# Attention units feeding a two-layer network: eight units scale their coarse probabilities on ScalarE, and a planner orders all work with a transfer rate of 400 GB/s

## The chip, the cores and the metric

One core of one Trainium2 chip. The metric is the device time of one execution in microseconds (us); the median of three runs is compared. Five engines work side by side, each through its own queue in a fixed order: TensorE (PE, with its weight loads PEld), VectorE (DVE), ScalarE (ACT), GpSimd (POOL) and SyncE (SP), which here issues every transfer.

## The reference

Attention over 4 batches of 8 heads (576 positions, 64 wide) is the sum of two parts: a coarse one on sums of four neighbours, and a local one with a band mask. Its output goes through a network of 512 to 2048 to 512 with the function h * tanh(softplus(h)).

```python
q_d = q.reshape(B, H, Sd, factor, D).mean(axis=3)      # factor = 4, k_d and v_d alike
out_up = np.repeat(sm_attn(q_d, k_d, v_d), factor, axis=2)
mask = np.abs(pos[:, None] - pos[None, :]) < factor
scores = np.where(mask, scale * np.matmul(q, k.transpose(0, 1, 3, 2)), -1e9)
x = out_up + softmax(scores) @ v                       # then to (2304, 512)
h = x @ w_in
g = h * np.tanh(np.log1p(np.exp(h)))                   # h itself above 20
return g @ w_out
```

## The kernel before

**Units.** Two heads make a unit; there are 16, named by batch b and pair p (0_0 to 3_3). A unit loads `qk` and `vv`, sums its q and k over fours on DVE (L347), and makes coarse scores `sc` (L362) and local scores `sl` (L397, for batches 0 and 1 with the mask added by a matmul, L392). The coarse exponentials are three ACT instructions (L369); the division by their sum is either three ACT instructions (L377, for units listed in `AMUL`) or one DVE instruction (L380). The local exponentials are either nine small ACT instructions with their sums (L407, units in `AEXP`, after two DVE steps L403 and L405) or one long ACT instruction (L417) between DVE steps L414, L415 and L418. Then PE transposes (`at` L443, `pt` L467, L473), multiplies with the coarse values (`pvo` L456, which needs POOL's sums `vd`, L430 and L432) and with the local values (`pve`, `pvo`, L482), and DVE and ACT put the sum into `x` as two fp32r parts (L495, L507, L509).

**Slots.** The network runs in 96 slots: a chunk c of 384 rows times one block f of 128 of the 2048 columns. A slot is 12 matmuls into `h` (L569), a chain between ACT and DVE (L583, L584, L586, L587, L589, L590, L593, L595) that ends with `g`, and 9 matmuls into three accumulators `acc` (L608, three for each). The first 32 slots run over chunks 0 and 1 together, chunk 1 behind chunk 0 by `LEAD` blocks; there the weights `wi` and `wo` of each block are loaded into `stg` and turned into two parts, with two ACT and four DVE instructions each (L541, L542, L544, L547, L550, L551). Chunks 2 to 5 use the weights that lie there, and units of batches 2 and 3 run among their slots, with one buffer each for `qk` and `vv`. The first six units have three buffer sets and a fourth, shared with all later units; the slots' PSUM is opened when those six are done.

**Order.** Nothing of it is written by hand. A planner in the kernel walks through a model of the engines, takes the ready operation with the lowest priority number, and writes each engine's order down. Priorities come from `ATT`, `UNIT`, `WPRI`, `VOFF`, `WDMA` (units, weights, transfers) and `LAG` (how many slots behind h the matmuls into acc come: slots below 20, below 60, the rest). `RATE` is the bandwidth by which it expects transfers to land:

```python
op("sp", P * 18 * 512 / RATE, lambda: nc.sync.dma_start(vv(), self.vv[b, p]), w=[vv], prio=pv_)
...
op("pe", 700, mm2, r=[*gi, wo], w=[a_], cols=1536, prio=s + LAG[(s >= 20) + (s >= 60)] - 0.5 + 0.1 * i)
```

Where PE has nothing ready, the planner may put in matmuls on constants (L695, into `warm` or into the unused end of an h buffer). On the chip the order is fixed, and each instruction waits for its own data.

Of the kernel before, what the change touches and what calls it, by code (L numbers as in the profile page):

```python
# [19 lines left out]
P = 128  # L20
BIG = 1e30
CH = 384
LAG = (3.5, 5.5, 5.5)
FA = 5
SETS = 3
ATT = {0: (-900, 20), 1: (-46, 10.0), 2: (5, 13.0), 3: (34, 5.5)}
WPRI = (9.1, 2.2, 7.7)
UNIT = {(0, 0): -3, (0, 1): -5, (0, 2): -2, (0, 3): -3, (1, 0): 5, (1, 1): -1, (1, 3): 1, (2, 0): -2, (2, 1): -1, (2, 2): 5, (2, 3): 2, (3, 0): 4, (3, 1): 2, (3, 2): 3, (3, 3): -2, (1, 2): -2}
WARM = True
NPRO = 6  # L30
STICK = 15
VOFF = 40
WDMA = 0
PIPE0 = (1, 0, 1)
PIPE1 = (1, 0, 1)
LEAD = 1
PMASK = (0, 1)
AMUL = ((0, 2), (1, 2))
AEXP = ((0, 1), (0, 2), (0, 3), (1, 1))
NMISH = (3, 2)  # L40
TAIL = 0
TICK, BUSY, PACE = 3413.3, 3060, 1.6
KW = 38
RATE = 280.0
DQ = 2500
ENGINES = ("pe", "act", "dve", "pool", "sp")
LATENCY = {"pe": (0, 197, 196, 272, 634), "act": (215, 143, 142, 170, 645), "dve": (240, 128, 127, 180, 620),
# [31 lines left out]
class Plan:  # L79
# [6 lines left out]
    def buf(self, group, tag, shape, dtype=F32, bufs=1, name=None):  # L86
        return Buf(self, group, tag, shape, dtype, bufs, name or f"{tag}_{len(self.ops)}")
# [183 lines left out]
def dve(n, fast=False):  # L271
    return 69 + (0.52 if fast else 1.042) * n


def act(n, psum=False, extra=0):
    return (52 if psum else 94) + 0.833 * n + 93 * extra
# [6 lines left out]
class Kernel:  # L283
# [45 lines left out]
    def attention(self, b, p, sb, ps, L, loose):  # L329
# [15 lines left out]
        qk, qkd = buf("qk", [P, 2, S + 6]), buf("qkd", [P, 2 * C])  # L345
        op("sp", P * 8 * (S + 6) / RATE, lambda: nc.sync.dma_start(qk(), self.qk[b, p]), w=[qk])
        op("dve", dve(2 * S), lambda: nc.vector.tensor_reduce(  # L347
# [26 lines left out]
        op("dve", 88, lambda: nc.vector.reciprocal(cst()[:, 3], cst()[:, 2]), w=[cst])  # L374
        if (b, p) in AMUL:
            for m in range(3):
# [24 lines left out]
        wide = lambda i: lst()[:, i, :, None].broadcast_to([P, T, KW])  # L401
        if (b, p) in AEXP:
            op("dve", dve(T * KW), lambda: nc.vector.tensor_reduce(out=lst()[:, 0], in_=sl3(), op=ALU.max, axis=AX.X),  # L403
# [20 lines left out]

        pv_ = pl.prio + VOFF
        vv, vd = buf("vv", [P, 18, P]), buf("vd", [72, 2, P])
        op("sp", P * 18 * 512 / RATE, lambda: nc.sync.dma_start(vv(), self.vv[b, p]), w=[vv], prio=pv_)
        vw = lambda: vv()[:, :10].rearrange("p (t f) c -> p t f c", f=2)
# [95 lines left out]
    def load_w(self, f):  # L524
# [6 lines left out]
        for nm, src in (("wi", wi), ("wo", wo)):  # L531
            pl.prio = prio + (WPRI[2] if nm == "wo" else 0)
            st_ = pl.buf("stg", "stg", [P, 512, 2], I32, self.nstg, f"stg_{nm}{f}")
# [4 lines left out]
            tmp = pl.buf("stg", "tmp", [P, 512], I32, 1, f"tmp_{nm}{f}")  # L538
            op("sp", P * 4096 / RATE, lambda st_=st_, src=src: nc.sync.dma_start(
                st_().rearrange("p (c f) w -> p c (f w)", c=4), src), w=[st_], prio=pl.prio + WDMA)  # L540
            op("act", act(512), lambda hf=hf: nc.scalar.activation(hf(), hf(), AF.Copy, scale=2.0 ** -112), w=[h])  # L541
# [14 lines left out]
    def slot(self, s, c, f):  # L556
# [46 lines left out]
        for i in range(3):  # L603
# [7 lines left out]
            gi = [g] if len(parts) == 1 else [(g, 2 * i), (g, 2 * i + 1)]  # L611
            op("pe", 700, mm2, r=[*gi, wo], w=[a_], cols=1536, prio=s + LAG[(s >= 20) + (s >= 60)] - 0.5 + 0.1 * i)
            if not last:
# [8 lines left out]
            r0 = c * CH + i * P  # L622
            op("sp", P * 2048 / RATE, lambda r0=r0, o=o: nc.sync.dma_start(self.out[r0:r0 + P, :], o()[:, :512]), r=[o], prio=s + 1)

    def run(self, ctx):
# [28 lines left out]
        for b in (0, 1):  # L654
            for p in range(self.NPAIR):
                if len(units) == NPRO:
                    break
                units.append((ATT[b][0] + ATT[b][1] * p + UNIT.get((b, p), 0), self.attention(
                    b, p, sets[len(units) % len(sets)], ("props", "attps"),
# [100 lines left out]
```

## Time and profile before

| what | value |
|---|---|
| median of 3 runs | 531.98 us (529.66 to 532.99) |
| the profiled execution | 531.69 us |
| its span, first to last instruction | 529.9 us |
| PE busy, share of the span | 511.8 us, 97% |
| DVE busy | 325.3 us, 61% |
| ACT busy | 356.8 us, 67% |

Matmuls are pipelined, so a busy PE is not PE at its peak: the matmuls on constants count as busy, and so does work at the lower clock. Shares over the whole span mix three stages: units alone, units and weights beside slots, and slots alone.

### The profile page before, as it was taken

To read this page: it belongs to the slowest core of one execution; us is meant where nothing else is said; L and a number is where in the kernel's file an instruction comes from. 1 tells how busy PE (TensorE), PEld (TensorE's weight loads), DVE (VectorE), ACT (ScalarE), POOL (GpSimd) and SP (SyncE) were. 2 spreads that over 40 slices of the span, in tenths; PEclk is the share of its full clock that TensorE was granted. 3 is DMA by queue.
4 is the path that set the end of the run, shared out by engine and by line. 5 is a ranking of instruction groups with operands and counts; after the bars stand their busy time and mean duration, and the time that the engine had idled before them with its cause. 6 is when DMAs were issued, how large, how long until landed. Compare 5 with 4: busy or idle time off the path is not lost.

```text
span 529.9 us, 11811 instructions
## 1 busy us (share of the span) xinstructions
PE 511.8 (97%) x4919; PEld 440.0 (83%) x4919; DVE 325.3 (61%) x686; ACT 356.8 (67%) x865; POOL 39.9 (8%) x54
## 2 busy tenths in 40 slices
PE   7889989999999999999999999999999999999997
PEld 3667777989899898878888788798989899898985
DVE  6677999999999633677745978543333333334242
ACT  3666778898889867667566566656566665666653
POOL 5430121000000000011200211100000000000000
PEclk9798999999999999999999999999999999999999
DMA  8763465434554000433303333100001000010001
GB/s 343 288 266 122 141 212 208 160 119 160 162 157 160 0 1 17 149 137 136 137 1 131 138 139 112 42 1 1 0 0 61 1 0 1 0 62 0 1 0 59
DMA packets 11861, 50.66 MB, mean 96 GB/s; under 512 B 1312, under 2 KB 1312, under 8 KB 9760
## 3 DMA queue, kind: packets, MB, share of 16 engines
q1 hardware_dynamic: 11808, 49.91, 26.4%
q8 instruction: 38, 0.62, 0.5%
q14 instruction: 15, 0.12, 0.1%
HBM read 45.19 MB, written 4.72 MB: 94 GB/s over the span
## 4 chain that ended last, share of the span: by engine, by line
PE 63%; DVE 4%; issue 1%; ACT 1%; POOL 0%
PE h L569 29%; PE acc L608 28%; PE pve L482 1%; PE sl L397 1%; PE sc L362 1%; PE pvo L456 1%; PE pt L467 1%; PE at L443 1%; PE pvo L482 1%; DVE g L595 1%; DVE mH L590 0%; DVE A L380 0%; DVE lst L418 0%; POOL vv L430 0%; DVE stg_wo L547 0%
## 5 line engine op out<-in xcount | busy, mean ns | idle before, releaser
L569 PE MATMUL h<-x,wi 128*128 128x384 f32 x1152 | 222.9, 340 | 1.9 <-DVE mH L590 1.6
L608 PE MATMUL acc<-wo,g 128*128 128x512 f32 x864 | 216.7, 395 | 0.5 <-DVE g L595 0.5
L569 PEld LDWEIGHTS h<-x,wi 128*128 128x128 f32 x1152 | 200.8, 188 | 14.7 <-DVE mH L590 6.8
L608 PEld LDWEIGHTS acc<-wo,g 128*128 128x128 f32 x864 | 160.5, 188 | 30.5 <-DVE g L595 0.9
L584 DVE TENSOR_SCALAR mA<-mA 128x384 f32<-128x384 f32 (+1 forms) x98 | 35.6, 364 | 95.3 <-ACT mA L583 95.3
L595 DVE SCALAR_TENSOR_TENSOR g<-mH,g 128x384 fp32r<-128x384 f32 (+1 forms) x98 | 56.2, 575 | 57.9 <-ACT g L593 57.9
L583 ACT ACTIVATE mA<-h 128x384 f32<-128x384 f32 (+1 forms) x98 | 46.8, 480 | 56.5 <-PE h L569 55.2
L586 ACT ACTIVATE mA<-mA 128x384 f32<-128x384 f32 (+1 forms) x98 | 50.6, 517 | 33.3 <-DVE mA L584 32.9
L593 ACT ACTIVATE g<-mH 128x384 fp32r<-128x384 f32 (+1 forms) x98 | 50.2, 514 | 16.2 <-PE acc L608 14.9
L587 ACT ACTIVATE mA<-mA,one 128x384 f32<-128x384 f32 (+1 forms) x98 | 59.0, 603 | 1.5
L590 DVE SCALAR_TENSOR_TENSOR mH<-mA,h 128x384 f32<-128x384 f32 (+1 forms) x98 | 53.1, 543 | 3.1 <-ACT mA L589 0.9
L589 ACT ACTIVATE mA<-mA 128x384 f32<-128x384 f32 (+1 forms) x98 | 50.4, 516 | 2.3
L430 POOL TENSOR_TENSOR vv<-vv 72x512 f32<-72x512 f32 x16 | 21.2, 1325 | 291.9 <-PE acc L608 176.4
L369 ACT ACTIVATE A<-sc,cst 128x144 f32<-128x144 f32 x48 | 17.9, 377 | 15.2 <-DVE cst L367 15.1
L482 PEld LDWEIGHTS pve<-PT,vv 38*64 38x64 f32 x640 | 21.1, 136 | 6.3 <-issue 3.4
L482 PE MATMUL pve<-PT,vv 38*64 38x32 f32 x640 | 23.0, 221 | 2.4 <-issue 2.4
L347 DVE TENSOR_REDUCE qkd<-qk 128x288 f32<-128x1152 f32 x16 | 21.5, 1343 | 4.6 <-DMA qk<-in_qk_dram 4.5
L397 PEld LDWEIGHTS sl<-qk 64*32 64x32 f32 x1152 | 13.2, 114 | 6.8 <-issue 5.3
L495 DVE TENSOR_TENSOR x<-pve,xd 128x320 f32<-128x320 f32 x16 | 7.8, 489 | 17.5 <-PE pve L482 17.3
L695 PE MATMUL warm<-ident 128*128 128x512 bf16 x56 | 17.0, 433 | 1.6 <-POOL ident masks.py:199 1.6
L482 PE MATMUL pvo<-PT,vv 38*64 38x32 f32 x512 | 18.4, 222 | 0.0
L507 ACT ACTIVATE x<-x 128x384 fp32r<-128x384 f32 (+1 forms) x32 | 12.4, 437 | 8.7 <-DVE x L495 8.7
(74 smaller groups left out, 460.6 us busy)
## 6 DMA issues: line engine op xcount, KB each, us to landing
vv<-in_vv_dram SPq DMA_DIRECT2D x16, 1152.0 KB, 5.8
qk<-in_qk_dram SPq DMA_DIRECT2D x16, 582.0 KB, 5.7
stg_wi<-in_w_in_dram SPq DMA_DIRECT2D x16, 512.0 KB, 3.4
stg_wo<-in_w_out_dram SPq DMA_DIRECT2D x16, 512.0 KB, 3.7
out_dram<-o SPq DMA_DIRECT2D x18, 256.0 KB, 2.1
```

Of the source, the lines that this page charges most:

```text
L347: op("dve", dve(2 * S), lambda: nc.vector.tensor_reduce(out=qkd().rearrange("p (a t) -> p a t", a=2), in_=qk()[:, :, 3:3 + S].rearrange("p ...
L482: nc.tensor.matmul(o_()[64 * h:64 * h + 64, c0:c0 + 32], vw()[64 * e:64 * e + KW, t // 2, f, 64 * h:64 * h + 64], PT()[64 * e:64 * e + KW, ...
L569: nc.tensor.matmul(h()[:, :CH], w()[:, a, kt * P:(kt + 1) * P], x()[:, b_, :], start=kt == 0 and j == 0, stop=kt == 3 and j == 2)
L583: op("act", act(n, True), lambda o_=o_: nc.scalar.activation(A()[:, o_], h()[:, o_], AF.Exp), r=[h_], w=[a_])
L584: op("dve", dve(n, True), lambda o_=o_: nc.vector.tensor_scalar(A()[:, o_], A()[:, o_], float(math.exp(20.0)), 1.0, op0=ALU.min, op1=ALU.a ...
L586: op("act", act(n), lambda o_=o_: nc.scalar.activation(A()[:, o_], A()[:, o_], AF.Square), w=[a_])
L587: op("act", act(n, False, 1), lambda o_=o_: nc.scalar.activation(A()[:, o_], A()[:, o_], AF.Ln, bias=self.one), w=[a_])
L589: op("act", act(n), lambda o_=o_: nc.scalar.activation(A()[:, o_], A()[:, o_], AF.Exp, scale=-1.0), w=[a_])
L590: op("dve", dve(n), lambda o_=o_: nc.vector.scalar_tensor_tensor(out=H()[:, o_], in0=A()[:, o_], scalar=0.5, in1=h()[:, o_], op0=ALU.subtr ...
L593: op("act", act(n), lambda o_=o_: nc.scalar.activation(g()[:, 0, o_], H()[:, o_], AF.Copy, scale=-2.0), r=[x_], w=[one])
L595: op("dve", dve(n), lambda o_=o_: nc.vector.scalar_tensor_tensor(out=g()[:, 1, o_], in0=H()[:, o_], scalar=-2.0, in1=g()[:, 0, o_].bitcast ...
L608: nc.tensor.matmul(a_(), g()[:, a, i * P:(i + 1) * P], wo()[:, b_], start=first and j == 0, stop=last and j == 2)
```

## The change

Only constants at the head of the file are changed. The first eight units (batches 0 and 1) all scale their coarse probabilities on ACT (`AMUL`), two units instead of four make their local exponentials in small ACT instructions (`AEXP`), and the numbers that set priorities and the transfer rate are others, so that the planner writes another order. The instructions of a slot, of a weight block and of the units of batches 2 and 3 stay the same.

```diff
-LAG = (3.5, 5.5, 5.5)
+LAG = (2.5, 5.0, 4.5)
...
-ATT = {0: (-900, 20), 1: (-46, 10.0), 2: (5, 13.0), 3: (34, 5.5)}
-WPRI = (9.1, 2.2, 7.7)
+ATT = {0: (-900, 20), 1: (-46, 10.0), 2: (5, 13.0), 3: (-34.40956924936998, 8.52050951677553)}
+WPRI = (10.326569533908831, 2.2, 1.3072351415990624)
...
-VOFF = 40
-WDMA = 0
+VOFF = 10
+WDMA = 3
...
-LEAD = 1
+LEAD = 2
...
-AMUL = ((0, 2), (1, 2))
-AEXP = ((0, 1), (0, 2), (0, 3), (1, 1))
+AMUL = ((0, 0), (0, 1), (0, 2), (0, 3), (1, 0), (1, 1), (1, 2), (1, 3))
+AEXP = ((0, 0), (1, 2))
...
-RATE = 280.0
+RATE = 400.0
```

`UNIT` changes for (0, 0), (0, 2), (0, 3) and (3, 2). The matmuls on constants go from 56 to 33 (`warm`) and from 39 to 14 (into h).

**The head of SP's queue.** A name holds batch, pair and a running number: `vv1_2` is the vv of unit 1_2. Before:

```order
L346 DMA qk0_0_116<-in_qk_dram 128x1164
L346 DMA qk0_1_119<-in_qk_dram 128x1164
L427 DMA vv0_0_130<-in_vv_dram 128x2304
L346 DMA qk0_2_187<-in_qk_dram 128x1164
...
L427 DMA vv1_1_815<-in_vv_dram 128x2304
L539 DMA stg_wi0_905<-in_w_in_dram 128x1024
L427 DMA vv1_2_969<-in_vv_dram 128x2304
L346 DMA qk1_3_1068<-in_qk_dram 128x1164
L539 DMA stg_wo0_1103<-in_w_out_dram 128x1024
L539 DMA stg_wi1_1164<-in_w_in_dram 128x1024
```

and of the change:

```order
L346 DMA qk0_0_116<-in_qk_dram 128x1164
L427 DMA vv0_0_118<-in_vv_dram 128x2304
L346 DMA qk0_1_132<-in_qk_dram 128x1164
L427 DMA vv0_1_177<-in_vv_dram 128x2304
L346 DMA qk0_2_192<-in_qk_dram 128x1164
...
L539 DMA stg_wi0_624<-in_w_in_dram 128x1024
L539 DMA stg_wo0_640<-in_w_out_dram 128x1024
L427 DMA vv1_1_662<-in_vv_dram 128x2304
L539 DMA stg_wi1_742<-in_w_in_dram 128x1024
L427 DMA vv1_2_900<-in_vv_dram 128x2304
L346 DMA qk1_3_978<-in_qk_dram 128x1164
```

Each vv of the first units now stands straight behind its own qk and ahead of the next one's; wo0 and wi1 moved ahead of vv1_2, which waits for a buffer of unit 0_3.

**PE between the h of slot 8 and the first acc of slot 8** (`h9` is the h of slot 9, `g8` the g of slot 8). Before:

```order
L569 MATMUL h8_1780<-x3_1_963,wi3_1646 128x384 x3
L608 MATMUL acc0_1_1521<-wo3_1678,g5_1745 128x512 x3
...
L608 MATMUL acc2_2_1652<-wo2_1592,g6_1778 128x512 x3
L569 MATMUL h9_1841<-x0_0_449,wi5_1792 128x384 x3
...
L608 MATMUL acc0_0_1510<-wo4_1739,g7_1839 128x512 x3
L569 MATMUL h10_1877<-x0_1_491,wi4_1717 128x384 x3
...
L608 MATMUL acc0_1_1521<-wo4_1739,g7_1839 128x512 x3
L608 MATMUL acc0_2_1529<-wo4_1739,g7_1839 128x512 x3
L608 MATMUL acc2_0_1635<-wo3_1678,g8_1864 128x512 x3
```

and of the change:

```order
L569 MATMUL h8_1751<-x3_0_951,wi5_1697 128x384 x3
L608 MATMUL acc0_1_1431<-wo4_1679,g6_1748 128x512 x3
L608 MATMUL acc0_2_1444<-wo4_1679,g6_1748 128x512 x3
L569 MATMUL h9_1797<-x0_1_501,wi3_1524 128x384 x3
L569 MATMUL h9_1797<-x1_1_674,wi3_1524 128x384 x3
L608 MATMUL acc3_0_1629<-wo2_1484,g7_1794 128x512 x3
L569 MATMUL h9_1797<-x2_1_809,wi3_1524 128x384 x3
L569 MATMUL h9_1797<-x3_1_956,wi3_1524 128x384 x3
L608 MATMUL acc3_1_1642<-wo2_1484,g7_1794 128x512 x3
L608 MATMUL acc3_2_1652<-wo2_1484,g7_1794 128x512 x3
L569 MATMUL h10_1843<-x0_0_488,wi6_1788 128x384 x3
L608 MATMUL acc0_0_1388<-wo5_1742,g8_1832 128x512 x3
```

Before, eight acc rows and eight h rows lie between the last h8 and the first use of g8; now five acc rows and five h rows do.

**PE between the end of unit 2_0 and `pvo` of unit 2_1.** Before:

```order
L482 MATMUL pve2_0_3048<-PT2_0_3053,vv2_0_1515 64x32 x4
L362 MATMUL sc2_1_3101<-qkd2_1_3032 64x144 x6
L397 MATMUL sl2_1_3114<-qk2_1_2981 32x38 x36
L608 MATMUL acc32_2_3158<-wo0_1335,g32_2897 128x512 x3
...
L608 MATMUL acc32_0_2995<-wo2_1592,g34_3174 128x512 x3
L569 MATMUL h38_3198<-x0_2_1105,wi6_1850 128x384 x3
...
L443 MATMUL at1_2_1_3215<-ident_59,A2_1_3165 72x128 x3
L569 MATMUL h38_3198<-x2_2_1327,wi6_1850 128x384 x3
...
L569 MATMUL h39_3232<-x0_2_1105,wi7_1933 128x384 x3
L456 MATMUL pvo2_1_3240<-AT02_1_3220,vd2_1_3227 64x144 x2
```

and of the change:

```order
L482 MATMUL pve2_0_3005<-PT2_0_3010,vv2_0_1536 64x32 x4
L362 MATMUL sc2_1_3052<-qkd2_1_2965 64x144 x6
L397 MATMUL sl2_1_3064<-qk2_1_2931 32x38 x36
L569 MATMUL h37_2981<-x3_2_1547,wi5_1697 128x384 x3
L608 MATMUL acc32_0_2945<-wo1_1235,g33_2874 128x512 x3
...
L569 MATMUL h38_3140<-x0_2_1073,wi6_1788 128x384 x3
L569 MATMUL h38_3140<-x1_2_1156,wi6_1788 128x384 x3
...
L443 MATMUL at1_2_1_3159<-ident_59,A2_1_3114 72x128 x3
L569 MATMUL h38_3140<-x2_2_1373,wi6_1788 128x384 x3
L569 MATMUL h38_3140<-x3_2_1547,wi6_1788 128x384 x3
L456 MATMUL pvo2_1_3181<-AT02_1_3164,vd2_1_3169 64x144 x2
```

Before, five acc rows and five h rows of slots lie between the two; now three acc rows and five h rows do.

## Rows read from the trace of the kernel before

**Rows 1.** The page: busy time by engine, and two transfers by size and landing.

```profile
PE 511.8 (97%) x4919; PEld 440.0 (83%) x4919; DVE 325.3 (61%) x686; ACT 356.8 (67%) x865; POOL 39.9 (8%) x54
...
vv<-in_vv_dram SPq DMA_DIRECT2D x16, 1152.0 KB, 5.8
qk<-in_qk_dram SPq DMA_DIRECT2D x16, 582.0 KB, 5.7
```

**Rows 2.** Windows by stage: length, busy PE, PEld, DVE, ACT, POOL, clock, DMA, GB/s.

```profile
4.50:62.00 57.50, 51.37 (x1206) 36.64 (x1205) 44.25 (x105) 36.24 (x169) 15.42 (x22) 0.91 0.62 243
62.00:93.00 31.00, 28.07 (x384) 23.77 (x383) 30.25 (x62) 24.36 (x56) 5.30 (x4) 1.00 0.56 197
93.00:219.00 126.00, 125.94 (x631) 113.17 (x630) 95.62 (x192) 103.13 (x207) 0.00 (x0) 1.00 0.32 103
219.00:340.00 121.00, 117.46 (x1774) 99.03 (x1774) 86.96 (x188) 75.03 (x200) 15.39 (x14) 1.00 0.33 118
340.00:516.00 176.00, 176.00 (x884) 158.45 (x884) 64.44 (x132) 111.36 (x218) 0.00 (x0) 1.00 0.03 10
```

**Rows 3.** The same view, two stretches of 10 us.

```profile
10.00:20.00 10.00, 7.14 (x171) 5.30 (x169) 8.12 (x24) 9.06 (x50) 4.08 (x5) 1.00 1.02 418
20.00:30.00 10.00, 8.91 (x199) 6.92 (x200) 5.50 (x15) 5.41 (x26) 2.73 (x4) 0.66 0.53 202
```

**Rows 4.** Chain that ended last: start, length, what; two slots apart.

```profile
371.04 2.11 PE h L569 x12
...
379.44 2.11 PE h L569 x12
```

**Rows 5.** Timeline of PE: start, length, instruction, idle time before and releaser.

```profile
21.09 0.32 PE L482 MATMUL pve<-PT,vv 38*64 38x32 f32 x2 [2.42 <-issue]
...
39.35 0.46 PE L456 MATMUL pvo<-AT,vd 72*64 72x144 f32 x2 [1.80 <-issue]
...
46.09 0.25 PE L482 MATMUL pve<-PT,vv 38*64 38x32 f32 x2
...
65.07 1.32 PE L569 MATMUL h<-x,wi 128*128 128x384 f32 x6
...
93.22 4.47 PE L569 MATMUL h<-x,wi 128*128 128x384 f32 x24
```

**Rows 6.** Timeline of POOL: vv of units 0_3 and 1_2 landed just before.

```profile
21.65 1.27 POOL L430 TENSOR_TENSOR vv<-vv 72x512 f32<-72x512 f32 x1 [0.84 <-DMA vv<-in_vv_dram]
...
52.95 1.26 POOL L430 TENSOR_TENSOR vv<-vv 72x512 f32<-72x512 f32 x1 [13.87 <-DMA vv<-in_vv_dram]
```

**Rows 7.** Groups by line of DVE in 0 to 93 us: busy us, mean ns.

```profile
L509 DVE TENSOR_TENSOR x<-x,x 128x384 fp32r<-128x384 f32 (+1 forms) x16 | 8.1, 545 | 0.1
...
L380 DVE TENSOR_TENSOR A<-A,cst 128x432 f32<-128x432 f32 x6 | 3.6, 596 | 0.1
...
L415 DVE TENSOR_TENSOR L_att<-sl,lst 128x342 f32<-128x342 f32 x4 | 2.0, 502 | 0.0
L418 DVE TENSOR_REDUCE lst<-L_att 128x9 f32<-128x342 f32 x4 | 2.0, 495 | 0.0
```

**Rows 8.** Groups by line and shape of ACT, whole span.

```profile
L407 ACT ACTIVATE L_att<-sl,lst 128x38 f32<-128x38 f32 x36 | 10.3, 296 | 0.0
...
L377 ACT ACTIVATE A<-A,cst 128x144 f32<-128x144 f32 x6 | 2.0, 407 | 0.5 <-DVE cst L374 0.5
```

**Rows 9.** Tile vv in 205 to 345 us: durations min/median/max, and landing.

```profile
L430 POOL TENSOR_TENSOR vv<-vv x7: 1282/1294/1382, 235.7 to 331.8; 72x512 f32<-72x512 f32 x7
L432 POOL TENSOR_TENSOR vd<-vv x7: 723/930/1043, 237.1 to 333.2; 72x256 f32<-72x256 f32 x7
...
DMA to landing us min/median/max: 5.0/5.2/7.0
```

**Rows 10.** Timeline of PE: the h of slot 12.

```profile
120.97 2.27 PE L569 MATMUL h<-x,wi 128*128 128x384 f32 x12
```

**Rows 11.** Timeline of DVE: the g of slot 12.

```profile
130.24 0.55 DVE L595 SCALAR_TENSOR_TENSOR g<-mH,g 128x384 fp32r<-128x384 f32 x1
```

More of the change, by code (lines that the diff above doesn't have):

```diff
@@ L22 @@
 CH = 384
-LAG = (3.5, 5.5, 5.5)
+LAG = (2.5, 5.0, 4.5)
 FA = 5
 SETS = 3
-ATT = {0: (-900, 20), 1: (-46, 10.0), 2: (5, 13.0), 3: (34, 5.5)}
-WPRI = (9.1, 2.2, 7.7)
-UNIT = {(0, 0): -3, (0, 1): -5, (0, 2): -2, (0, 3): -3, (1, 0): 5, (1, 1): -1, (1, 3): 1, (2, 0): -2, (2, 1): -1, (2, 2): 5, (2, 3): 2, (3, 0): 4, (3, 1): 2, (3, 2): 3, (3, 3): -2, (1, 2): -2}
+ATT = {0: (-900, 20), 1: (-46, 10.0), 2: (5, 13.0), 3: (-34.40956924936998, 8.52050951677553)}
+WPRI = (10.326569533908831, 2.2, 1.3072351415990624)
+UNIT = {(0, 0): 1, (0, 1): -5, (0, 2): 1, (0, 3): -1, (1, 0): 5, (1, 1): -1, (1, 3): 1, (2, 0): -2, (2, 1): -1, (2, 2): 5, (2, 3): 2, (3, 0): 4, (3, 1): 2, (3, 2): 4, (3, 3): -2, (1, 2): -2}
 WARM = True
```

## The prediction

> **What bounds the kernel now.** The page comes first: PE is busy 97% of the span and DVE 61% [rows 1], which looks like a PE limit throughout. The windows by stage correct that [rows 2, 3]. From 340 to 516 us PE is busy all the time and DVE a third of it: slots alone, nothing to win by an order. A pair of slots starts every 8.40 us there, a slot costs 4.2 us, its four h rows 2.11 us and its nine acc matmuls (three rows of 0.70) the rest [rows 4]. From 93 to 219 us PE is busy too (125.94 of 126.00). From 219 to 340 us it is idle for 3.5 us. What is lost lies ahead of 93 us. The first h starts only at 65.07 us and the first that runs on without a gap at 93.22 us [rows 5]. By then PE has done the eight first units, five h and ten acc rows. Many of the busy microseconds there are matmuls on constants.
>
> In that first stage DVE is what comes last. It is busy 44.25 of 57.5 us from 4.5 to 62 us and 30.25 of 31 us from 62 to 93 us [rows 2]: 74.5 us of work and 14.0 us of idling, nearly all of it early, and then a queue that never empties until weight block 3 is ready and the slots can run on. So the start is set by DVE's early idle time. It waits there for PE and ACT: PE stands 2.42 us in the middle of unit 0_0 and 1.80 us in unit 0_3, both with nothing but its own issue as releaser [rows 5], and behind the first of these the granted clock falls to 0.66 for 10 us [rows 3]. Unit 0_3 multiplies with its values at 46.09 us although its vv landed by 21.65 us [rows 5, 6]; unit 1_2 shares its buffer, so its vv lands only at 52.95 us, and wo0 and wi1 stand behind that transfer in SP's queue.
>
> **The change part by part.** *Scaling on ACT, fewer exponentials on ACT.* Up to weight block 3, six L380 go (6 x 0.596 = 3.6 us of DVE [rows 7]). Two units leave `AEXP` on balance: each gains L415 and L418 (1.0 us) and drops the short L405 (I take 0.2 us), +1.6 us together [rows 7]. ACT gets 18 more L377 (7.3 us) and loses 18 L407 (5.3 us and their sums) for two long L417 [rows 8]. It is busy 36.24 of 57.5 us there [rows 2], so it takes this, and its queue loses the long runs of nine L407 behind which other units waited. By DVE's order, weight block 3 is also reached with seven instructions fewer of x, weights and slots (two each of L509 and L584, one each of L542, L590 and L595); L509 is 0.545 us [rows 7], the others no longer, so I take 3.3 us. DVE's work to that point is 74.5 - 3.6 + 1.6 - 3.3 = 69.2 us.
>
> *The order of the first 93 us.* Transfers really land at the rate that the planner now assumes: 418 GB/s while the queue is full [rows 3], so 2.8 us for a vv of 1152 KB and 1.4 us for a qk of 582 KB [rows 1]. Since each vv goes ahead of the next qk, the second qk lands about 2.8 us later than before and the third at some 13 to 14.5 us, and DVE waits for it: I put 2.5 us. Unit 0_0 then multiplies with its values at about 20 us, since in the new order that stands behind the third unit's scores. From there a unit costs DVE some 5.5 us (up to 62 us it did seven units and one weight tile in 44.25 us [rows 2], about 6 each, and 0.6 us of that is L380), and transfers are ahead: unit 0_1 at 26, 0_2 at 31 and 0_3 at 36 us (before 46.09). Then vv of 1_2 goes out, lands 5.2 us later [rows 9] at some 42 us (before 52.95), and wo0 and wi1 no longer stand behind it. The first h starts near 50 us.
>
> So DVE's finish with block 3 is 4.5 us (its start) + 69.2 us + idle time. For the idle time I add 2.5 us for the third qk, 1 us at the first units, when only two are under way, and 2 us for unplanned PE stops of the kind that the trace shows: 5.5 us, against 14.0. That gives 79.2 us. PE has then done one h and three acc rows less than at 93.22 us before, 2.1 + 2.1 = 4.2 us. At equal work the start is at 83.4 us instead of 93.2: **9.8 us gained**. Ends: with 2 us idle 13.3, with 11 us (four fifths of before) 4.3; if all idle time stays it is 1.3.
>
> The Trainium skill's page "DMA: Bandwidth & Descriptors" (section "Where 436 GB/s comes from") has about 358 GB/s per core bind for reads from HBM; the trace's 418 GB/s disagrees. By that figure the first ten transfers, 8.3 MB, would end 3.3 us later (an estimate), and the gain would be nearer 7 us.
>
> *Behind the start.* With `LEAD` 2 block 4 is wanted a slot earlier; between blocks 3 and 4 DVE has 17 rows, some 8.5 us at half a microsecond each as L509's [rows 7], and PE eight h and five acc rows, 8 x 0.53 + 5 x 0.70 = 7.7 us: +1 us (0 to 2).
>
> *LAG 2.5.* In slots 2 to 19 the first acc of a slot now comes after about five acc and five h rows (6.1 us; where the order gives more, 7.7), before it was eight and eight (9.8). The chain took 7.55 us in slot 12, from h's end at 123.24 us to g's at 130.79 [rows 10, 11], but part of that was waiting behind weight rows of both engines, which the new order mostly puts elsewhere. An acc that waits delays the chain of every second slot, so of 18 slots nine waits add up. At the chain of before the spacing is short by 1.4 to nothing, 0.7 on the mean: +6 us, the upper end; the lower is 0. I take +1 us, a chain about as long as its spacing.
>
> *The middle.* In 219 to 340 us a unit's vv goes out when the unit before has used its buffer, and `vd` is ready 5.2 + 1.29 + 0.93 = 7.4 us later [rows 9]. The new order, which expects the transfer to be faster, leaves eight acc and four h rows less between these two points, summed over six units: 8 x 0.70 + 4 x 0.53 = 7.7 us less cover. PE idled only 3.5 us in the whole stage before [rows 2], so cover was rarely short; I take +1 us, ends -1 and +4. Slots alone and the end stay.
>
> The sum is -9.8 + 1 + 1 + 1 = -6.8 us. The profiled execution took 531.69 us, 1.8 us over its span and 0.3 us under the median; 531.98 - 6.8 gives **525.0 us** rounded.
>
> **The rivals.** *Slower, by late g's:* the chain stays long because the weights keep both engines full (DVE 95.62 of 126 us there [rows 2]). At 8.5 us against a mean spacing of 6.6 us, nine waits of 1.9 us cost 17 us, and with 9.8 us gained and 2 us elsewhere the kernel takes 541 us. It turns slower than before once a wait is over 0.9 us. Against it: PE was fully busy in that stage, and the weights are done well before the slots that need them.
>
> *No change, by a cold PE and early stops:* 23 of 56 `warm` matmuls and 25 of 39 into h go. A window at 0.66 of the clock costs PE 3.4 us in ten [rows 3], and DVE waits for PE; two more such stretches leave 3 us of the gain, 530 us. The same time results if the order does not hold on the chip and only the work moved off DVE counts. The Trainium skill speaks for it: in "TensorE: Matmul & The Clock Gate" ("What's actually happening") the lower clock is the default and activity lifts it; the trace agrees, as the clock fell behind a stop of 2.42 us. For the forecast: units come closer together and fill PE themselves.
>
> *A larger gain:* no stops, every wait as planned: 13.3 us from the start and the other terms at zero, 518 us.
>
> **How the numbers follow.** Forecast 45%, no change 25%, slower 15%, larger gain 15%. Over 1% (5.3 us, about what can be told from no change here) faster are the larger gain, most of the forecast and a little of the no-change case: 0.58; slower is most of the slower case, 0.15; the rest 0.27. The range 516.5 to 534.5 leaves out the worst of the late g's and a start better than the walk.
>
> **What would show it.** First h near 50 us and the gapless run from near 80 us; DVE over 85% busy from 15 to 80 us; fourth unit's values near 36 us; PE waits of some tenths before acc in slots 4 to 19; waits for `vd` between 219 and 330 us; the stage of slots alone unchanged. The prediction is wrong if DVE idles over 10 us before block 3, or if PE waits for g by a microsecond in most slots.

## The result, and the profile after

The changed kernel takes 534.02 us in the median of 16 executions, the kernel before 529.98 us beside it. The ratio is 1.0075, with a 95% interval of 1.0046 to 1.0103: slower by 0.75%, where 525.0 us had been forecast. Medians, here and below, are over all executions; the ratios leave out those that the record calls slow, here one of the 16 at 1707 us.

The profiled execution does not show this gap by itself: 532.18 us after, 531.69 us before. Executions of one program differ by up to 9 us here, and the two profiled ones lie on opposite sides of their medians. So the trace tells where time is lost, and several traces of the same order are needed to tell how much.

Of the page after, the busy time and the line on the engines' own instruction transfers (packets, MB, share):

```profile
PE 503.8 (95%) x4871; PEld 436.3 (82%) x4871; DVE 319.5 (60%) x682; ACT 356.8 (67%) x849; POOL 40.4 (8%) x54
...
q8 instruction: 38, 0.62, 0.5%
```

The windows by stage, to be laid beside [rows 2], three stretches of 10 us beside [rows 3], and the stretch up to the end of `wi` of block 3, which DVE finishes at 83.16 us:

```profile
4.50:62.00 57.50, 46.27 (x1192) 34.93 (x1191) 46.60 (x110) 40.02 (x156) 16.12 (x22) 0.94 0.68 259
62.00:93.00 31.00, 28.30 (x364) 23.76 (x363) 29.28 (x63) 25.09 (x61) 4.86 (x4) 1.00 0.56 199
93.00:219.00 126.00, 125.25 (x702) 112.02 (x701) 93.58 (x186) 102.93 (x203) 0.00 (x0) 1.00 0.29 99
219.00:340.00 121.00, 114.45 (x1687) 97.05 (x1687) 83.04 (x188) 73.65 (x200) 15.64 (x14) 1.00 0.32 113
340.00:516.00 176.00, 176.00 (x882) 159.09 (x881) 62.87 (x129) 108.00 (x214) 0.00 (x0) 1.00 0.03 10
...
10.00:20.00 10.00, 7.75 (x183) 5.68 (x184) 9.37 (x25) 7.37 (x28) 3.98 (x4) 1.00 1.01 415
20.00:30.00 10.00, 8.00 (x255) 6.49 (x255) 7.61 (x18) 6.49 (x25) 3.63 (x3) 0.83 0.88 319
30.00:40.00 10.00, 7.38 (x126) 5.80 (x126) 6.70 (x17) 4.68 (x16) 2.49 (x3) 0.83 0.64 231
...
4.50:83.17 78.67, 65.15 (x1507) 50.46 (x1506) 67.52 (x155) 57.93 (x200) 18.63 (x24) 0.96 0.63 234
...
82.48 0.68 DVE L551 TENSOR_TENSOR wi<-stg_wi,wi 128x512 fp32r<-128x512 f32 x1
```

Two things are to be seen. DVE, which was to be idle for 5.5 us ahead of weight block 3, is idle for 11.2 us up to there (78.67 - 67.52), where it was 14.0 before. That is over the 10 us that the prediction named as a sign of being wrong. And PE is idle for 6.55 us between 219 and 340 us, where it was 3.54 us [rows 2]. The stage of slots alone is unchanged, as forecast.

The timeline of PE, to be laid beside [rows 5] (start, length, instruction, idle time before and releaser):

```profile
21.70 0.24 PE L482 MATMUL pvo<-PT,vv 38*64 38x32 f32 x2 [1.83 <-issue]
...
32.21 0.19 PE L482 MATMUL pvo<-PT,vv 38*64 38x32 f32 x1 [2.51 <-issue]
...
41.16 0.60 PE L467 MATMUL pt<-ident,L_att 128*128 128x128 f32 x4 [1.57 <-DVE cst L367]
...
43.91 0.24 PE L482 MATMUL pve<-PT,vv 38*64 38x32 f32 x1
...
60.31 2.35 PE L569 MATMUL h<-x,wi 128*128 128x384 f32 x12
...
77.18 0.71 PE L456 MATMUL pvo<-AT,vd 72*64 72x144 f32 x8 [1.94 <-POOL vd L432]
...
89.15 1.83 PE L569 MATMUL h<-x,wi 128*128 128x384 f32 x9 [0.41 <-DVE mH L590]
```

Unit 0_0 multiplies with its values at 18.7 us, near the walk's 20. Unit 0_3 does so at 43.91 us instead of 36, the first h starts at 60.31 us instead of 50, and the run without gaps begins at about 89 us instead of 80. In between stand stops of PE of 1.83, 2.51 and 1.57 us. The first two have "issue" as releaser: PE waited for nothing that a semaphore shows. The clock is 0.83 in both stretches behind them, a mean of its two levels, 1.2 and 2.4 GHz.

Unit 1_2 gets its vv later than forecast too (42 us); POOL's sums over it begin at 51.07 us, hardly ahead of before [rows 6]:

```profile
51.07 1.84 POOL L430 TENSOR_TENSOR vv<-vv 72x512 f32<-72x512 f32 x1 [10.85 <-DMA vv<-in_vv_dram]
```

In the middle stage the waits of PE (total, times, longest) are led by vd, which before was waited for once, for 0.8 us; the transfers of vv there land after 5.0 to 6.7 us, median 5.5 (before 5.0 to 7.0, median 5.2 [rows 9]):

```profile
PE pvo L456 <- POOL vd L432: 3.1, 5, 1.1
PE h L569 <- DVE mH L590: 1.2, 1, 1.2
...
DMA to landing us min/median/max: 5.0/5.5/6.7
```

**What an "issue" stop is.** The number of PE's instructions that the profile has ahead of such a stop is one of a few, in every trace. The windows from 0 to the end of the three stops after (PE and PEld with their counts):

```profile
0.00:21.69 21.69, 14.20 (x349) 8.97 (x350) 13.60 (x29) 12.08 (x50) 10.96 (x28) 1.00 0.93 373
0.00:32.20 32.20, 22.20 (x604) 15.46 (x605) 21.78 (x46) 17.44 (x69) 15.31 (x32) 0.95 0.89 347
0.00:41.15 41.15, 29.58 (x730) 21.26 (x731) 28.42 (x64) 23.14 (x87) 17.31 (x34) 0.92 0.82 314
```

That is 699, 1209 and 1461 instructions; before, the stops at 21.09 and 39.35 us [rows 5] come after 698 and 1458. From one to the next they differ by 252 or by two or three times 253 to 255. The page says what lies between them: 38 transfers of kind "instruction" on one queue, 0.62 MB, so 16 KB each (15 more on another queue have 8 KB each), and 9742 instructions of PE and PEld over 38 are blocks of 256 each (a few records are missing in a trace). The second stop begins at 29.70 us, and the view of transfers finds its block only behind 29.8 us, while the queue for data is full. First 27.7 to 29.8 us, then 29.8 to 31 us:

```profile
q1 hardware_dynamic: 195, 0.77, 97.6%
```

```profile
q1 hardware_dynamic: 127, 0.46, 94.9%
q8 instruction: 1, 0.02, 4.6%
```

PE goes on at 32.21 us, behind that packet. So the reading is: PE has run to the border of a block, and the next block is fetched late, behind data. The kept traces bear it out: ahead of 100 us there are 22 stops of over 0.8 us at such a border, in thirteen of the fourteen traces (thin has none), and at each of them PE goes on 1.2 to 1.6 us behind the end of that border's packet. That the third stop (releaser "cst") lies on a border as well, and goes on 1.3 us behind its packet, shows that the releaser alone does not tell.

The Trainium skill's page "Runtime: NRT & Kernel Launch" (section "Instruction fetch mechanics") has each engine refill its instructions in blocks of 16 KiB, or 256 instructions, over a queue of its own while it works on the block before, at a cost that is "mostly hidden". The traces agree on the blocks and disagree on the cost, here up to 3.5 us a border.

### The profile page after: what moved, and what is told of

Same layout as the page of the kernel before. It is cut to its first block, busy times and chain, and to the rows that moved or that the text cites. A ratio compares the mean times of both kernels' runs of the same rounds, so it can differ in the third digit from the quotient of the medians.

```text
span 530.4 us, 11781 instructions
## 1 busy us (share of the span) xinstructions
PE 503.8 (95%) x4871; PEld 436.3 (82%) x4871; DVE 319.5 (60%) x682; ACT 356.8 (67%) x849; POOL 40.4 (8%) x54
## 4 chain that ended last, share of the span: by engine, by line
PE 59%; DVE 6%; DMA 3%; POOL 1%; ACT 1%; issue 1%; POOLq 0%; DVEq 0%; SPq 0%
PE acc L608 27%; PE h L569 26%; DMA qk<-in_qk_dram 2%; PE pve L482 1%; DMA vv<-in_vv_dram 1%; POOL vv L430 1%; PE pt L467 1%; PE sc L362 1%; PE pvo L456 1%; PE sl L397 1%; PE pvo L482 1%; DVE mH L590 1%; DVE qkd L347 1%; PE at L443 0%; DVE g L595 0%
## 5 line engine op out<-in xcount | busy, mean ns | idle before, releaser
L569 PE MATMUL h<-x,wi 128*128 128x384 f32 x1152 | 226.2, 340 | 2.6 <-DVE mH L590 2.3
L608 PE MATMUL acc<-wo,g 128*128 128x512 f32 x864 | 221.2, 395 | 0.0
L569 PEld LDWEIGHTS h<-x,wi 128*128 128x128 f32 x1152 | 203.1, 188 | 15.4 <-DVE mH L590 5.0
L595 DVE SCALAR_TENSOR_TENSOR g<-mH,g 128x384 fp32r<-128x384 f32 (+1 forms) x98 | 53.5, 547 | 82.9 <-ACT g L593 82.7
L586 ACT ACTIVATE mA<-mA 128x384 f32<-128x384 f32 (+1 forms) x98 | 50.5, 517 | 37.8 <-DVE mA L584 37.5
L584 DVE TENSOR_SCALAR mA<-mA 128x384 f32<-128x384 f32 (+1 forms) x98 | 34.8, 356 | 57.7 <-ACT mA L583 57.5
L430 POOL TENSOR_TENSOR vv<-vv 72x512 f32<-72x512 f32 x16 | 22.1, 1384 | 290.7 <-PE at L443 155.4
L482 PE MATMUL pvo<-PT,vv 38*64 38x32 f32 x512 | 18.7, 221 | 4.5 <-issue 4.5
L397 PEld LDWEIGHTS sl<-qk 64*32 64x32 f32 x1152 | 12.0, 108 | 7.8 <-DMA qk<-in_qk_dram 5.1
L482 PEld LDWEIGHTS pvo<-PT,vv 38*64 38x64 f32 x512 | 16.6, 133 | 2.2 <-issue 2.2
```

The source lines that it names most:

```text
L430: op("pool", gps(512), lambda: nc.gpsimd.tensor_tensor(out=vc()[:, :, 0:2], in0=vc()[:, :, 0:2], in1=vc()[:, :, 2:4], op=ALU.add), w=[(vv, ...
L482: nc.tensor.matmul(o_()[64 * h:64 * h + 64, c0:c0 + 32], vw()[64 * e:64 * e + KW, t // 2, f, 64 * h:64 * h + 64], PT()[64 * e:64 * e + KW, ...
L569: nc.tensor.matmul(h()[:, :CH], w()[:, a, kt * P:(kt + 1) * P], x()[:, b_, :], start=kt == 0 and j == 0, stop=kt == 3 and j == 2)
L584: op("dve", dve(n, True), lambda o_=o_: nc.vector.tensor_scalar(A()[:, o_], A()[:, o_], float(math.exp(20.0)), 1.0, op0=ALU.min, op1=ALU.a ...
L586: op("act", act(n), lambda o_=o_: nc.scalar.activation(A()[:, o_], A()[:, o_], AF.Square), w=[a_])
L595: op("dve", dve(n), lambda o_=o_: nc.vector.scalar_tensor_tensor(out=g()[:, 1, o_], in0=H()[:, o_], scalar=-2.0, in1=g()[:, 0, o_].bitcast ...
```

## The experiments

**How the traces are compared.** "Lost" is the time less the work that PE has done by then, counted by its instructions: an h row 0.53 us, an acc row 0.70 us, all of a unit's PE instructions 4.9 us (4.6 without the mask), matmuls on constants nothing (these prices are rounded). Every version does 478.9 us of such work. The third column of times ends with PE's last matmul, 3.7 us ahead of the span's end. Lost time in us:

| profiled execution | to 100 us | 100 to 219 | 219 to PE's end | clock | span |
|---|---|---|---|---|---|
| before | 36.9 | 0.8 | 9.6 | 0.989 | 529.9 |
| before_again | 34.7 | 0.8 | 8.6 | 0.993 | 526.7 |
| rest_new | 37.8 | 0.6 | 14.5 | 0.986 | 535.5 |
| after | 33.7 | 1.9 | 12.2 | 0.994 | 530.4 |
| after_again | 35.2 | 2.0 | 12.4 | 0.986 | 532.3 |
| start_new | 34.5 | 3.0 | 9.4 | 0.990 | 529.5 |
| rate_280 | 39.2 | 1.2 | 8.8 | 0.987 | 531.8 |
| div_only | 41.3 | 0.9 | 9.2 | 0.986 | 534.0 |
| gate_before | 32.4 | 0.7 | 9.7 | 0.997 | 525.3 |
| gate2 | 32.3 | 0.4 | 10.1 | 1.000 | 525.3 |
| gate3 | 32.6 | 0.9 | 10.0 | 0.999 | 526.1 |
| thin | 29.1 | 2.2 | 14.4 | 0.990 | 528.4 |
| gate_after | 39.8 | 2.6 | 13.1 | 0.979 | 538.2 |
| pvo_later | 38.2 | 1.7 | 16.3 | 0.975 | 538.8 |

**1. Halves of the change: start_new and rest_new.** The numbers for batches 0 and 1 and the weights from one kernel, those for batches 2 and 3 and the later slots from the other. The edits here and below are shortened.

```diff
 # start_new, against the change
-LAG = (2.5, 5.0, 4.5)
+LAG = (2.5, 5.5, 5.5)
-3: (-34.40956924936998, 8.52050951677553)
+3: (34, 5.5)
+RATE2, VOFF2 = 280.0, 40
-op("sp", P * 18 * 512 / RATE, ...
+op("sp", P * 18 * 512 / (RATE if b < 2 else RATE2), ...
```

> The change's order for batches 0 and 1, the weights and the first 20 slots (with its transfer rate, AMUL and AEXP); the numbers of the kernel before for batches 2 and 3, for slots from 20 on and for the rate that their transfers are planned with. Theory A (the start gains some 3 us, the middle loses it again): against before at the same clock 3 us faster, about 527 us, ratio 0.994; PE idle between 219 and 340 us back to about 3.5 us. Theory B (the gap between the medians comes from the start itself, which has fewer matmuls on constants and so a lower granted clock in many executions): slower than before, 533 us or more, ratio over 1.005, granted clock mostly under 0.99.

> The other half: the start of before, the change's numbers for batches 2 and 3 and slots from 20 on. Theory A: 3 us slower than before, about 533 us, ratio 1.006, with some 6 us of PE idle between 219 and 340 us and waits for vd in most units. Theory B: within 1 us of before, ratio 0.998 to 1.002.

start_new: 533.0 us against 529.57 us, ratio 1.0086 (1.0051 to 1.0121). rest_new: 535.89 us, ratio 1.0125 (1.007 to 1.018). Both halves are slower than before. The windows of the middle stage, start_new first, separate its part cleanly:

```profile
219.00:340.00 121.00, 116.89 (x1775) 99.31 (x1775) 82.80 (x188) 74.88 (x201) 15.74 (x14) 1.00 0.33 118
```

```profile
219.00:340.00 121.00, 112.98 (x1689) 95.61 (x1688) 82.66 (x184) 73.61 (x199) 15.27 (x14) 1.00 0.33 118
```

PE is idle for 4.1 us with the old numbers and 8.0 us with the new ones. So theory A holds for the middle. For the start it falls: the new start with the old middle is not 3 us faster but 3.4 us slower in the median. Theory B's clock is seen as well: 0.9865 on the mean of start_new's executions, 0.9932 on before's. The number of matmuls on constants does not explain it, as rate_280 shows. In start_new's profiled execution the stop behind 1209 instructions is longer still:

```profile
31.00 0.19 PE L482 MATMUL pvo<-PT,vv 38*64 38x32 f32 x1 [3.48 <-issue]
```

The halves do not add up: 3.4 and 6.3 us more in the medians, 4.0 for the whole change. For rest_new the middle is not all: in the start that it shares with before it has a third stop at a border, behind 2219 instructions, which before does not have.

```profile
54.81 1.09 PE L467 MATMUL pt<-ident,L_att 128*128 128x128 f32 x4 [2.47 <-DVE x L509]
```

What each half costs by itself is therefore not shown by these times, only the idle time of PE in the middle.

**2. Parts of the change: div_only and rate_280.**

```diff
 # div_only, against before
-AMUL = ((0, 2), (1, 2))
-AEXP = ((0, 1), (0, 2), (0, 3), (1, 1))
+AMUL = ((0, 0), (0, 1), (0, 2), (0, 3), (1, 0), (1, 1), (1, 2), (1, 3))
+AEXP = ((0, 0), (1, 2))
 # rate_280, against the change
-RATE = 400.0
+RATE = 280.0
```

> Before with the change's AMUL and AEXP alone. If DVE's work sets the start, 2 us less of it (3.6 less 1.6) show as 1 to 3 us: 527 to 529 us, ratio 0.994 to 0.998. If the start is set by stops of PE and by what ACT does, nothing: ratio 0.998 to 1.002, and DVE is idle longer before 93 us by as much as its work is shorter.

> The change with the transfer rate of before, 280 GB/s, and all else as changed. If the rate is what takes the cover away before vd: PE idle between 219 and 340 us falls from 6.5 to about 4 us and the kernel takes 531 to 532 us. If the rate is what brought the gain of the start: the gapless run begins some 3 us later and it takes 536 us or more.

div_only: 535.53 us, ratio 1.0111 (1.0057 to 1.0164), worse than either theory. Two us less work on DVE bought nothing, since the new order that follows has stops of its own, one of 2.43 us at a border (38.02 us) and the longest just before the slots run on:

```profile
91.40 2.02 PE L569 MATMUL h<-x,wi 128*128 128x384 f32 x7 [4.45 <-DVE mH L590]
```

rate_280: 531.99 us, ratio 1.0066 (1.0033 to 1.0099). Between 219 and 340 us PE is idle for 1.65 us instead of 6.55, and from 219 us on it loses 8.8 us instead of 12.2: the rate is what took the cover away there. That the whole kernel is faster than as changed is not shown; the two intervals overlap.

```profile
62.00:93.00 31.00, 26.89 (x341) 23.11 (x338) 28.27 (x57) 22.35 (x53) 4.37 (x4) 0.83 0.62 216
...
219.00:340.00 121.00, 119.35 (x1715) 101.45 (x1713) 86.10 (x191) 77.28 (x207) 14.09 (x13) 1.00 0.33 118
```

Its start loses 39.2 us, more than as changed, with a stop of 3.26 us at the border behind 699 instructions (22.88 us), and with the clock at 0.83 from 62 to 93 us, where PE waits 2.26 us for vd of 1_3. It has 57 matmuls on constants into warm, start_new and the changed kernel 33, and its clock over 12 executions, 0.9863, is no higher than start_new's. So their number does not set the clock; in the traces it falls behind long stops.

**3. The stops themselves: gate_before, gate2, gate3.** Each engine but SP keeps before's order to the row. On SP a copy of one number waits for a result and so holds back the transfers behind it.

```diff
+HOLD = ((("vv", 0, 2), ("xd", 0, 0)), (("vv", 0, 3), ("xd", 0, 1)), (("vv", 1, 0), ("xd", 0, 2)), ...
+            def fn(fn=d.fn, src=src, k=k):
+                self.nc.sync.dma_start(self.held[:1, k:k + 1], src()[:1, :1])
+                fn()
 # gate2, against gate_before
-(("vv", 0, 2), ("xd", 0, 0))
+(("vv", 0, 2), ("x32", 0, 0))
 # gate3, against gate2
-(("vv", 0, 2), ("x32", 0, 0)) ... (("vv", 1, 0), ("xd", 0, 2)), (("vv", 1, 1), ("xd", 0, 3))
+(("vv", 0, 2), ("L", 0, 1)) ... (("vv", 1, 0), ("xd", 0, 3))
```

> The kernel before, with every instruction of PE, DVE, ACT and POOL in its old order; on SP's queue alone five transfers that are not needed yet are held back, each by a copy of one number that waits for a result (vv of 0_2 for the xd of 0_0, vv of 0_3 for that of 0_1, vv of 1_0 for that of 0_2, vv of 1_1 for that of 0_3, wo0 for that of 1_0). Theory C (PE runs out of instructions, because its next block of 16 KB is fetched behind the data transfers that are under way): the stops of 2.4 us in the values of 0_0 and of 1.8 us in pvo of 0_3 go or fall under 0.7 us, the clock stays at 1.0 more often (mean over 0.996), and the kernel takes 3 to 4 us less: 526 us, ratio 0.993. Rival D (the stops come from the dense runs of small matmuls or from the chain between PE, ACT and DVE, whatever the transfers do): the stops stay within 0.5 us of what they were, and the time is the same or, by transfers that come late, 1 to 2 us longer.

In gate_before the two stops of before [rows 5] are gone. One new "issue" stop of over 1 us stands at a border between them:

```profile
23.70 0.19 PE L482 MATMUL pve<-PT,vv 38*64 38x32 f32 x1 [1.70 <-issue]
```

The vv of 0_2 went out just ahead of that border's block. The view of transfers has data alone from 17.4 to 21.0 us, and the block, with six small packets beside it, from 21.0 to 22.2 us:

```profile
q1 hardware_dynamic: 139, 1.18, 90.8%
```

```profile
q8 instruction: 1, 0.02, 5.3%
...
q1 hardware_dynamic: 5, 0.00, 0.2%
```

Same instructions in the same order, other transfers under way, other stops at other borders: theory C holds for the stops, and rival D falls. The time: 527.92 us against 529.85 us, but ratio 0.9996 (0.9961 to 1.0031), so no gain is shown yet, and the mean clock is 0.994, where over 0.996 was expected.

> As the first kernel with held transfers (all engines but SP in the order of before), but the vv of 0_2 now waits for 0_0's sum of both parts (x32) instead of its xd, and so goes out some 3 us later, behind the fetch of the instruction block that it delayed there by 3.7 us. Theory C: the stop of 1.7 us at 22 us goes too, no stop with the releaser issue is over 0.7 us before 62 us, mean clock over 0.996, 525 to 527 us, ratio 0.990 to 0.995. Rival D (the stop of 22 us belongs to the dense run of small matmuls): it stays, and so does the time of the first such kernel, 528 to 529 us.

gate2: 527.22 us against 528.99 us, ratio 0.9967 (0.9941 to 0.9994), faster than before by 0.33%, less than the 0.5 to 1% expected, and with an interval that ends just under 1. The stop at 22 us is gone, and the clock stays at 1.00, on the mean of its executions 0.997:

```profile
4.50:62.00 57.50, 51.89 (x1337) 37.74 (x1337) 48.26 (x115) 40.01 (x180) 15.55 (x22) 1.00 0.68 252
```

Held too long, a transfer is waited for itself, and one border still has its stop:

```profile
27.55 0.71 PE L456 MATMUL pvo<-AT,vd 72*64 72x144 f32 x8 [1.51 <-POOL vd L432]
...
35.35 0.46 PE L456 MATMUL pvo<-AT,vd 72*64 72x144 f32 x2 [1.92 <-issue]
```

> As the second kernel with held transfers, the order of before on all engines but SP; the vv of 0_2 waits for 0_1's local probabilities (about 1 us earlier than in the second), the vv of 1_0 for the xd of 0_3 (some 5 us later), the vv of 0_3 and wo0 as there. Theory C: the wait of 1.5 us for vd of 0_2 shrinks to under 0.7 us, the stop of 1.9 us in pvo of 0_3 at 34 us goes, since no vv is ahead of its block any more, and the kernel takes 524 to 526 us, ratio 0.988 to 0.994. Rival D: the stop at 34 us stays, 527 us as in the second.

gate3: 528.8 us, ratio 0.9987 (0.9961 to 1.0013). The stop at 35 us falls to 0.3 us, but another of 1.5 us appears at the border at 45 us. The expected two to three us did not come.

**4. The forecast's walk without the data: thin.** The changed order on all engines but SP. Six transfers of vv are left out, their units read the values of 0_0 instead, and three transfers of weights go earlier.

```diff
+THIN = ((0, 1), (0, 2), (0, 3), (1, 0), (1, 1), (1, 2))
-lambda: nc.sync.dma_start(vv(), self.vv[b, p])
+lambda: None if (b, p) in THIN else nc.sync.dma_start(vv(), self.vv[b, p])
```

> The changed kernel, every instruction of PE, DVE, ACT and POOL in its order, with six transfers of vv left out (units 0_1 to 0_3 and 1_0 to 1_2 read the values of 0_0, so the output is not the reference's), and wi0, wo0 and wi1 sent earlier, in the places of two of them: from some 18 us on hardly any data moves. It asks whether the start that the forecast walked through lies in this order once PE's instruction blocks are not fetched behind data. Theory C: the stops at the borders of the blocks (2.5 to 3.5 us in the values of 0_1, 1.6 us before pt at 40 us) shrink to under 1 us each, unit 0_3's values come at 37 to 39 us (44 as changed, 36 forecast), the first h at 52 to 54 us (60.3), and the kernel takes 527 to 529 us. Rival G (the units of this order are spaced by the chain of PE, ACT and DVE, and other waits take the place of the stops): unit 0_3's values stay past 41 us, the first h past 57 us, and the kernel takes 531 to 534 us.

No stop at a border over 0.4 us is left ahead of 60 us. DVE is busy 54.09 of 57.5 us, and the units come as the prediction walked them (26, 31 and 36 us for the values of 0_1 to 0_3, 50 us for the first h). `wi` of block 3 is ready at 78.3 us (forecast 79.2) behind 5.9 us of idling (forecast 5.5):

```profile
4.50:62.00 57.50, 53.02 (x1308) 40.40 (x1306) 54.09 (x126) 45.14 (x170) 15.80 (x22) 0.97 0.41 152
4.50:78.30 73.80, 66.28 (x1507) 51.71 (x1506) 67.92 (x155) 56.84 (x200) 18.41 (x24) 0.95 0.41 153
```

```profile
27.73 0.25 PE L482 MATMUL pve<-PT,vv 38*64 38x32 f32 x2
...
32.47 0.24 PE L482 MATMUL pve<-PT,vv 38*64 38x32 f32 x1
...
37.69 0.24 PE L482 MATMUL pve<-PT,vv 38*64 38x32 f32 x1
...
53.55 2.35 PE L569 MATMUL h<-x,wi 128*128 128x384 f32 x12
...
71.05 1.00 PE L456 MATMUL pvo<-AT,vd 72*64 72x144 f32 x8 [3.04 <-POOL vd L432]
```

29.1 us are lost to 100 us, 7.4 less than the mean of the three traces with the old start (36.5). The time, 529.26 us, ratio 0.9999 (0.997 to 1.0027), is just over the range expected: the wait for vd of 1_3 grew to 3.04 us and the middle loses 14.4 us. DVE's waits for PE's values, as changed and then in thin, show what went:

```profile
DVE x L495 <- PE pve L482: 4.7, 4, 1.7
```

```profile
DVE x L495 <- PE pve L482: 0.8, 1, 0.8
```

Units 0_1 to 0_3 wait for no vv of their own here either, so not all of the 7.4 us need be the blocks'.

**5. Two repairs that failed: gate_after and pvo_later.** The first holds back three transfers of the changed kernel, the second puts pvo of nine units two slot rows later on PE.

```diff
 # gate_after
+HOLD = ((("vv", 0, 3), ("xd", 0, 0)), (("qk", 1, 2), ("xd", 0, 2)), (("vv", 1, 1), ("xd", 0, 3)))
 # pvo_later
+for j in [j for j in range(i, len(pe)) if pe[j].deps is not None and pe[j].cols in (1152, 1536)][:2]:
+    pe.insert(i, pe.pop(j))
```

> The changed kernel, all engines but SP in its order; three transfers are held back in the same way (vv of 0_3 for the xd of 0_0; qk of 1_2, and so wi0 and wo0 behind it, for the xd of 0_2; vv of 1_1 and wi1 for the xd of 0_3). Theory C: the stops in the values of 0_1 (2.5 us) and before pt at 41 us (1.6 us) go or fall under 0.7 us, unit 0_3's values come at about 38 us instead of 44, the first h some 4 us earlier, and the kernel takes 529 to 530 us, ratio to before 0.999 to 1.002. Rival D: stops and milestones stay within 1 us, 533 to 535 us.

543.2 us, ratio 1.023 (1.0155 to 1.0305). wi0 landed late behind the held qk, and ACT's step on it stood in ACT's queue ahead of the copy that PE needed:

```profile
PE sl L392 <- ACT AT L448: 3.6, 1, 3.6
```

A stop of 1.9 us behind 1209 instructions stayed. At a time this much longer the run speaks neither for C nor for D; it shows what a held transfer costs.

> The changed kernel; on PE alone, pvo of 1_3 and of the eight units of batches 2 and 3 (with what stands behind it in the unit up to there) stands two rows of h or acc later, so that vd has 1.1 to 1.4 us longer; all other queues as changed. Theory E (vd is late because the order counts on 400 GB/s, while a vv that goes alone takes 5 to 6.5 us to land): waits of pvo for vd fall from 5.0 us in all to under 1.5 us, the stop of 1.9 us at 75 us falls to about 0.6 us, and the kernel takes 530 to 531.5 us (2.5 to 4 us less than as changed), ratio to before 1.000 to 1.004. Rival F (PE's time is only moved: the rows taken forward then wait for their own g and h): PE idle from 219 to 340 us stays over 5.5 us, and 533 to 535 us.

539.9 us, ratio 1.0188 (1.0143 to 1.0234). The waits for vd are gone from the list, and others stand in their place from 93 to 340 us, beside one of 3.5 us for mH at 76 us with the clock at 0.78 from 62 to 93 us:

```profile
PE pve L482 <- ACT PT L474: 3.9, 6, 0.7
PE h L569 <- DVE mH L590: 2.4, 4, 1.4
```

Theory E falls as a repair. Rival F holds for the idle time of PE from 219 to 340 us, 6.9 us, but the time is 5 us over what it had, with a stop of 3.5 us at the border behind 1209 instructions too. By the trace the wait for vd is only the first of a unit's steps that the new order places too close.

**6. The same kernels again: before_again and after_again.** Unchanged, one profiled execution each.

> The kernel before, unchanged, for a second profiled execution. If the time of an execution goes with its stops of PE and the clock behind them: the stops lie at the same borders of instruction blocks (in the values of 0_0, in pvo of 0_3, or at another border), but their lengths differ by a microsecond or more; where all are under 1 us the clock is at least 0.997 and the span under 527 us, where two are over 1.5 us it is 529 us or more. If execution times scatter for another reason: the same stops within 0.3 us, and a span that differs by over 1 us all the same.

> The changed kernel, unchanged, for a second profiled execution. By the same theory: the stop in the values of 0_1 at some 28 to 30 us again (2.5 us or more, as in three traces of this start), the wait for vd of 1_3 at 72 to 76 us again (1.4 us or more); the span is over 532 us if the clock falls behind both, 529 to 531 us if it falls behind one. The loss between 93 and 219 us again 1 to 3 us and the PE idle time between 219 and 340 us again 6 to 7 us.

528.61 us and 534.05 us. The waits of before_again with releaser "issue":

```profile
PE pve L482 <- issue: 2.2, 1, 2.2
...
PE pvo L456 <- issue: 1.3, 1, 1.3
```

and of after_again the stops behind 1209 and 1461 instructions:

```profile
30.97 0.19 PE L482 MATMUL pvo<-PT,vv 38*64 38x32 f32 x1 [1.99 <-issue]
...
39.36 0.60 PE L467 MATMUL pt<-ident,L_att 128*128 128x128 f32 x4 [2.58 <-DVE qkd L347]
```

The borders are the same, the lengths differ by up to 1 us. Between the two changed executions the second stop shortened by 0.5 us and the third grew by 1.0 us. With one stop over 1.5 us and one of 1.3 us, before_again lies between the two cases expected, and its span of 526.7 us nearer to the short one.

## Why the prediction was wrong

**The sum, term by term.** Three traces each (before, before_again and rest_new for the old start; after, after_again and start_new for the new one; for the rest before, before_again and start_new against after, after_again and rest_new):

| term | forecast | measured |
|---|---|---|
| start, to 100 us | -9.8 | 34.5 - 36.5 = -2.0 |
| behind the start and late g's, to 219 us | +1 +1 | 2.3 - 0.7 = +1.6 |
| middle, to the end | +1 (-1 to +4) | 13.0 - 9.2 = +3.8 |
| sum | -6.8 | +3.4 (medians +4.0) |

The first row is at the edge of the scatter: 33.7 to 35.2 us with the new start, 34.7 to 37.8 with the old. The three executions with the new start ran on the mean 1.2 us under the medians of their kernels, those with the old one 0.6 us over, and start_new's median is 3.4 us over that of before. A gain of the start is therefore not shown.

**The step that failed** is the idle time of DVE in the start, 5.5 us, and in it "2 us for unplanned PE stops of the kind that the trace shows". The trace before showed two such stops of 2.42 and 1.80 us with nothing but issue as releaser [rows 5], and the prediction put 2 us for them in the new order without asking where they come from. They belong to the borders of instruction blocks, which fall at fixed counts of instructions in any order. In the three traces of the new start the stops at borders of over 1 us come to 4.7 to 5.9 us instead of 2, and the clock falls behind them. That a start which packs units and transfers closer reaches a border sooner and with more data ahead of the block fits this, but is argued.

As changed, DVE was busy 67.5 us (forecast 69.2) and idle 11.2 us (forecast 5.5) up to `wi` of block 3, which is the end that the prediction's count of DVE's instructions leads to; it was ready at 83.2 us (forecast 79.2). With these two numbers the prediction's own sum gives 93.2 - 83.2 - 4.2 = 5.8 us. The 4.2 us were too little as well: at 83.2 us PE had done five h rows and nearly five acc rows less than at 93.22 us before, 5.9 us of work.

thin shows that the walk itself was near: with that data away, the values of 0_1 to 0_3 and the first h come within 1.5 to 3.6 us of the forecast, and 7.4 us of the 9.8 are there. That the total of 5.5 us is met in thin is in part luck: DVE never waits for the third qk, which was put at 2.5 us, and small waits for ACT and PE stand in its place.

**Transfers "at the rate that the planner now assumes"** was half right. A full queue does move 415 GB/s (10 to 20 us after; 418 before [rows 3]); the Trainium skill's "DMA: Bandwidth & Descriptors" ("Where 436 GB/s comes from") has about 358 as what binds for reads from HBM, and the trace disagrees again. But a vv that goes alone takes 5.0 to 6.7 us to land, which is 1152 KB at 176 to 236 GB/s. For the middle the old figure of 280 was nearer the truth, and rate_280 gives that stage back. The prediction had named this term and its bounds; it lies at +3.8 near their upper end (+4), and LAG and LEAD together came out 0.4 us under their 2.

**The cold PE** was a rival, put down to fewer matmuls on constants. What the runs show is that the clock falls behind stops, if not behind every one: in gate2, with a single "issue" stop of over 1 us ahead of 93 us, it is 1.00 in both windows. The Trainium skill's "TensorE: Matmul & The Clock Gate" ("What's actually happening") has the lower clock as the default that activity lifts; the traces agree (0.83 behind the stops of 1.83 and 2.51 us after). The changed kernel's executions run at 0.9887 on the mean and before's, beside start_new, at 0.9932, and an execution at 0.996 took 532.0 us where one at 0.978 took 539.4 us. What part of the 4 us is the clock's own and what the stops' is not separated here. Late g's, the rival on the slower side, are not in the trace: PE waits for no g in slots 4 to 19.

**Open:** why the length of a stop at the same border varies by a microsecond from one execution to the next, and whether the blocks wait for whole transfers or for a share of the queue.

## What to carry to other kernels

Where PE stops with nothing but issue as releaser, count its instructions up to each stop: if the counts differ by multiples of a block, look for the block's packet just ahead of where PE goes on. Such a stop is a fetch: it falls on a fixed count of instructions, and its length goes with the transfers under way. Hold back transfers that nobody needs yet, but only as long as nobody does; a held transfer is soon the next wait. Give a planner the time that a lone transfer takes to land, not the bandwidth of a full queue, and compare orders over several profiled executions: a difference of 3 us between two traces was within what one order shows by itself.

## What was not expected of the hardware

- PE's instructions come in 38 transfers of 16 KB, and behind data one of them cost PE up to 3.5 us at a border (start_new); in gate_before, one vv ahead of a block cost it 1.7 us.
- Five copies of one number each on SP's queue, each waiting for a result, were enough to move the stops of PE and to gain 0.33% with the work of all other engines unchanged (gate2).
- Small instructions of DVE stretch beside POOL's sums over vv: L372, 0.16 us by itself, took 1.24 us at 51.70 us after, while L430 ran on POOL. In that trace all nine DVE instructions ahead of 93 us that took over 0.15 us more than their median ran beside L430 or L432.
